# Block sums of the first 1024 tokens written straight into weight places, and single weight halves taken ahead of the last block

## The chip, the core and the metric

The kernel runs on one core of a Trainium2 chip. The metric is the device time of one execution in microseconds (us). TensorE (PE) does the matmuls, VectorE (DVE), ScalarE (ACT) and GpSimd (POOL) the elementwise work, and SyncE (SP) issues nearly all DMAs.

## What is computed

The reference has three stages in a row:

- a decaying linear attention over 4 sequences of 768 tokens, 8 heads of 64: state = gamma * state + k v^T, y = q state / 8. Its output is x, 3072 tokens by 512;
- layer 1: h = x @ w_in (512 to 2048), g = max(0.01 h, h), x2 = g @ w_out (2048 to 512);
- layer 2: h = x2 @ w_in2, g = h * cos(h), out = g @ w_out2, of the same sizes.

All of it is wanted at fp32 precision. A matmul operand is therefore split into a high part (rounded to the fp32r type) and a low part (the rest), and each product is three matmuls: high*high, low*high, high*low (`mm3`, lines 330 to 333).

## The kernel before

**Blocks and stages.** The 3072 tokens are six blocks of 512. Layer 1 runs over `SEGMENTS` (line 678): blocks 0 and 1 in two parts each, then n = 2, 3, 4, 5 whole. In a block, step f (0 to 15) does `gemm1` of 128 hidden features (12 matmuls), and then `gemm2_a` of step f-3 (12 matmuls), since up to two finished g wait in `pending`. After PE's gemm1 the value goes through ACT (`Leaky.begin`, then `high_g`) and DVE (`low_g`, line 541). The output of block n goes to DRAM tensors `x2d[n]`. Attention for the block after is woven into blocks up to n = 4; the last block, n = 5, has none.

**Layer 2** runs after that in 24 "quads" (lines 960 to 1005), eight for each superblock s of 1024 tokens (two blocks). It uses a 2 by 2 block scheme with seven products, P1 to P7, in the order P1, P6, P7, P5, P2, P4, P3. The left factors are sums of weight blocks, held per pair p in `w2i[p]` (DRAM) and loaded by `load_wi`; the right factors are sums of the x2 blocks, 14 tiles per superblock (seven names, two halves k), each a high part of 512 columns beside a low part of 512. They stand in `xt[j]`, in the places `w{j}_0` in which layer 1 has its input weights. Layer 2's output weights are rounded and split to `w2d[f]` (DRAM) and loaded by `load_wo`.

**Side work and its order.** Layer 2's operands are made while layer 1 runs. There are three kinds of such work, and every step of it has a *moment*, two per f: `agenda.run(2*(NF*(n-2)+f-START)+k)` in `tick` (line 800), with START = 4. Block n = 3 has moments 24 to 55, n = 4 has 56 to 87, and n = 5 has 88 to 119. Engines take their instructions in program order, so a moment fixes each engine's order.

- A **half** (`half(f)`, line 617) makes `w2d[f]`: one fetch of 512 KB, two ACT passes, three DVE passes (`clamp`, `fraction`, `top_bits`; lines 125, 128, 133), a POOL add (line 138), then `parts`: an ACT copy for the high part, a POOL subtraction for the low part, and a 256 KB write for each. It spans 7 moments, and the next begins 4 after it. Halves work in `cbuf`.
- A **pair** (`pair_at`, line 628) makes `w2i[p]`: two fetches of 512 KB, twice the rounding, four sums on DVE (`pair_sums`, line 266, 256 columns each), and four high and low parts, 1.8 MB of writes. Pairs 0 and 1 work in `cbuf`. Pairs 2 to 7 are those of `last_pairs`: they begin at moments 88, 92, ..., 108 in buffers of their own, the pool `ppool`, and take 10 moments each (the last ends at moment 118).
- **xprep** (line 276) makes the 14 x tiles of one superblock: for each k four fetches of 256 KB from `x2d` into `cbuf`, four sums on DVE, seven high parts on ACT (line 249), seven low parts on DVE (line 255), and a write of 256 KB to `xq[s]` for each part.

Before the change the order is: halves 0 to 7 (moments 0 to 34), pair 0 (32 to 44), xprep of s = 0 (46 to 70), pair 1 (69 to 81), halves 8 to 15 (80 to 114). So half 9's end and halves 10 to 15 run in the last block beside the six pairs. Also in the last block, `load_xq(0, f)` (line 813) brings one x tile of 512 KB from `xq[0]` back after each gemm1 of f = 0 to 13, `load_wo` brings 8 tiles of 512 KB, and `load_wi` 1.8 MB at f = 8 and again at f = 15.

**The crossing to layer 2.** `ppool` is closed and `bpool` opened in its room (line 842), so the first tile of `bpool` (`a`, copied by ACT at line 978 out of P1's bank) has to wait for the last DMA that reads a `ppool` tile. The products take their banks in turn: P1 and P6 two of `ps_h`, P7 `attA`, and P5 needs P1's bank again.

```python
650:            for f in range(8):
651:                half(f)
652:            pair(0)
653:            xprep(agenda, m + 3, 0)
654:            m += 26
655:            pair(1)
656:            for f in range(8, NF):
657:                half(f)
```

Of the kernel before, what the change touches and what calls it, by code (L numbers as in the profile page):

```python
# [12 lines left out]
F32 = mybir.dt.float32  # L13
F32R = mybir.dt.float32r
# [4 lines left out]
ALU = mybir.AluOpType  # L19
# [5 lines left out]
P = 128  # L25
# [7 lines left out]
NB = NT // BLK  # L33
# [24 lines left out]
WIN = 3584  # L58
WCOLS = {"P1": (0, 512), "P2": (256, 768), "P6": (1024, 1536), "P3": (1280, 1792), "P7": (2048, 2560), "P5": (2304, 2816), "P4": (3072, 3328)}
XORDER = ("P1", "P6", "P7", "P5", "P2", "P4", "P3")  # L60


def tables():
# [17 lines left out]
def body(ctx: ExitStack, tc: tile.TileContext, att, w1, w2, tab, out):  # L81
    nc = tc.nc
# [7 lines left out]
    dpool = ctx.enter_context(tc.tile_pool(name="dpool", bufs=1, space=DRAM))  # L90
# [19 lines left out]
    def w_tile(f, part, dt, n):  # L110
        return wpool.tile([P, n], dt, tag=f"w{f}_{part}", name=f"w{f}_{part}")
# [96 lines left out]

    w2d = [dpool.tile([P, 1024], F32, name=f"w2d{f}") for f in range(NF)]
    w2i = [dpool.tile([P, WIN], F32, name=f"w2i{p}") for p in range(NF // 2)]  # L210
    xq = [[dpool.tile([P, 1024], F32, name=f"xq{s}_{i}") for i in range(14)] for s in range(NB // 2)]
    made = set()


# [26 lines left out]

    def parts(t, dst, lo, eng, keep, out):

        o = []

        def high():
            n = t().shape[-1]
            o.append(out(n))
            nc.scalar.copy(out=o[0].bitcast(F32R), in_=t().bitcast(F32))
            nc.sync.dma_start(out=dst[:, lo : lo + n], in_=o[0])  # L250

        def low():
            n = t().shape[-1]
            w = out(n) if keep else t().bitcast(F32)
            eng.tensor_tensor(out=w.bitcast(F32R), in0=t().bitcast(F32), in1=o[0], op=ALU.subtract)
            nc.sync.dma_start(out=dst[:, lo + n : lo + 2 * n], in_=w)

        return high, low

# [13 lines left out]
    def done(*what):  # L273
        return lambda: made.add(what)

    def xprep(agenda, m, s):

        def place(i):
            return lambda: cbuf[:, i, :]

        def fetch(i, k):
            src = x2d[2 * s + i // 2][:, 2 * (i % 2) + k, :]
            nc.sync.dma_start(out=cbuf[:, i, :].bitcast(F32), in_=src)

        b11, b21, b12, b22 = (cbuf[:, i, :] for i in range(4))
        for k in range(2):
            way = {}
            for i, name, keep in ((0, "P1", True), (1, "P2", True), (3, "P3", True), (0, "P5", False), (2, "P7", False), (3, "P6", False), (1, "P4", False)):
                way[name] = parts(place(i), xq[s][2 * XORDER.index(name) + k], 0, nc.vector, keep, ostage)
            b = m + 13 * k  # L290
            for i in range(4):
                agenda.put(b + (0 if k == 0 else (-3, 0, -2, -1)[i]), partial(fetch, i, k))
            for j, name in ((2, "P1"), (3, "P2"), (4, "P3"), (6, "P5"), (7, "P7"), (8, "P6"), (9, "P4")):
                agenda.put(b + j, way[name][0])
                agenda.put(b + j + 1, way[name][1])
                if name == "P3":
                    agenda.put(b + 4, partial(sub2, b11, b12, b11))
                    agenda.put(b + 5, partial(sub2, b12, b22, b12))
                if name == "P5":
                    agenda.put(b + 6, partial(sub2, b22, b22, b11))  # L300
                    agenda.put(b + 7, partial(sub2, b21, b21, b22))
        agenda.put(m + 24, done("x", s))


    xt = {}

    def load_xq(s, j):
        assert ("x", s) in made
        xt[j] = w_tile(j, 0, F32R, 1024)
        nc.sync.dma_start(out=xt[j].bitcast(F32), in_=xq[s][j])  # L310

    wo = {}

# [230 lines left out]
    with tc.manual_schedule():  # L544

        with ExitStack() as pctx, ExitStack() as actx:
# [57 lines left out]
            agenda = Agenda()  # L604
            START, LAST = 4, 2 * (NF * (NB - 3) - 4)
# [11 lines left out]
            def half(f):  # L617
                nonlocal m, turn
                t = own(2 + turn % 2)
                turn += 1  # L620
                first, mid, last = rounding(raw2, t)
                high, low = parts(t, w2d[f], 0, nc.gpsimd, False, ostage)
                for i, step in enumerate((begin(f, 1), int, first, mid, last, high, low)):
                    agenda.put(m + i, step)
                agenda.put(m + 6, done("w", f))
                m += 4
# [15 lines left out]
            def pair(p):  # L642
                nonlocal m, turn
                t1, t2 = own(2 + turn % 2), own(3 - turn % 2)
                fetches = [begin(2 * p + i, 0) for i in range(2)]
                times = (0, 2, 3, 4, 4, 6, 7, 8, 5, 6, 9, 10, 10, 11, 11, 12, 12)
                pair_at(agenda, m, p, t1, t2, (raw2, raw2), fetches, times, (nc.gpsimd, nc.gpsimd, nc.vector), ostage, ostage)
                m += 11
# [1 line left out]
            for f in range(8):  # L650
                half(f)
            pair(0)
            xprep(agenda, m + 3, 0)
            m += 26
            pair(1)
            for f in range(8, NF):
                half(f)

            def last_pairs(ppool):
                def late(fn):  # L660
# [124 lines left out]
            for seg, (n, f0, f1) in enumerate(SEGMENTS):  # L785
                limit = LAG - 2 if seg < 4 else 1
                steps = list(PLAN[seg])
                size, at = len(steps), 0

                def slots(k):  # L790
                    for _ in range(size - len(steps), min(size, (k * size + size // 2) // (2 * (f1 - f0)))):
                        steps.pop(0)()

                def tick(k):
                    if seg < 4 and wa.busy() and k < int(TICKS[seg][f - f0]):
                        if loads and (seg > 0 or loads[0][0] < NF - 7):
                            load_w(1)
                        wa.tick()
                    if n > 1:
                        agenda.run(2 * (NF * (n - 2) + f - START) + k)  # L800

                for f in range(f0, f1):
                    if n == NB - 1 and f % 4 > 1:
                        hp = ps_att.tile([P, 512], F32, tag="attA" if f % 4 == 2 else "attB", name="hp")
                    else:
                        hp = ps_h.tile([P, 512], F32, tag="h", name="hp")
                    hp = hp[:, :BLK]
                    if len(pending) > limit:
                        need(wa, pending[0][2], 1)
                    need(wa, f, 0)  # L810
                    gemm1("a", f, xs[n], hp)
                    if n == NB - 1 and f < 14:
                        load_xq(0, f)
                    if n == NB - 1 and f == 8:
                        load_wi(0, 0)
                    if n == NB - 1 and f == NF - 1:
                        load_wi(1, 1)
                    if prev:
                        g = leaky.finish(*begun)
                        gh = high_g(g)  # L820
                    slots(2 * (f - f0) + 1)
                    tick(0)
                    second(limit)
                    if prev:
                        eng = nc.gpsimd if seg < 3 and GLP[seg][f - f0] == '1' else nc.vector
                        pending.append((gemm2_a, *prev[:2], low_g(g, gh, eng), *prev[2:]))
                    begun = leaky.begin(hp)
                    slots(2 * (f - f0) + 2)
                    tick(1)
                    prev = n, f, f0, f1  # L830
                if f1 == NF:
                    xs.pop(n)
                if n == NB - 2:
                    actx.close()
                    ppool = pctx.enter_context(tc.tile_pool(name="ppool", bufs=1))
                    last_pairs(ppool)
# [12 lines left out]
        def product(q, name):  # L849
            w = wi[pair_of(q)][0]  # L850
            hi, lo = WCOLS[name]
            at = XORDER.index(name)
            o = bank("attA") if (7 * q + at) % 3 == 2 else ps_h.tile([P, 512], F32, tag="h", name="hp")
            for k in range(2):
                j = 2 * at + k
                x = xt[j]
                mm3(o, w[:, hi + k * P : hi + k * P + P], w[:, lo + k * P : lo + k * P + P], x[:, :512], x[:, 512:], k == 0, k == 1)
                if q % NQ == NQ - 1 and q < QUADS - 1:
                    load_xq(q // NQ + 1, j)
            return o  # L860
# [86 lines left out]
        places = {f: f for f in range(8)}  # L947
        xagenda = Agenda()
        for s in range(1, NS):
            xprep(xagenda, 4 * NQ * (s - 1) + 1, s)  # L950
        moment = iter(range(4 * QUADS))

        def spare():
# [90 lines left out]
```

## Time and profile before

| | |
|---|---|
| median of 3 runs (range) | 1180.66 us (1179.08 to 1181.03) |
| the profiled execution | 1182.37 us, its span 1180.3 us |
| PE busy | 1129.1 us (96%), 5584 matmuls |
| DVE busy | 841.7 us (71%) |
| ACT busy | 525.9 us (45%) |
| POOL busy | 295.5 us (25%) |
| DMA moved | 204.82 MB, 174 GB/s over the span |
| mean granted TensorE clock | 0.991 |

The span is the time from the first to the last instruction in the trace; the execution's own time is 2.07 us more. The profile cuts the span into 40 slices of 29.5 us, with the busy share of each engine in tenths, the granted clock, and the DMA rate. A queue of DMA instructions on an engine is named SPq or ACTq.

### The profile page before, as it was taken

What the parts mean: (1) busy time and instruction counts of PE and PEld (TensorE: products, weight loads), DVE (VectorE), ACT (ScalarE), POOL (GpSimd) and SP (SyncE); (2) the same over time, 40 slices, a digit from 0 to 9 for tenths busy, and PEclk for the clock granted to TensorE, in tenths of its full rate; (3) what the DMA queues carried; (4) which work ended last, traced back from release to release, by engine and by line L of the source; (5) the groups of instructions that cost most, each with busy time, mean ns of one, the idle gap of its engine ahead of it and who ended that gap; (6) DMA issues with size and microseconds to landing.
All of it is one profiled execution on the core that took longest, in us unless ns stands there. A gap on an engine that the chain in (4) does not pass through costs nothing.

```text
span 1180.3 us, 15708 instructions
## 1 busy us (share of the span) xinstructions
PE 1129.1 (96%) x5584; PEld 929.6 (79%) x5584; DVE 841.7 (71%) x1313; ACT 525.9 (45%) x954; POOL 295.5 (25%) x274
## 2 busy tenths in 40 slices
PE   7889989999999999999987799999999999999998
PEld 5678778888888888888865577888888888888886
DVE  7899885444555655653797588798888897877875
ACT  4556543333334443334544354453445444444432
POOL 5687763222334421233455200000000000000000
PEclk9999999999999999999998899999999999999999
DMA  9905422223335344414999744648455567343321
GB/s 343 312 10 205 161 71 73 73 92 105 108 110 176 117 169 169 180 63 141 330 388 390 248 143 156 233 146 321 170 195 198 190 231 265 116 143 134 108 88 72
DMA packets 79854, 204.82 MB, mean 174 GB/s; under 512 B 8864, under 2 KB 13088, under 8 KB 79776
## 3 DMA queue, kind: packets, MB, share of 16 engines
q1 hardware_dynamic: 79632, 203.56, 48.9%
q8 instruction: 44, 0.72, 0.3%
q14 instruction: 34, 0.28, 0.1%
q10 hardware_dynamic: 144, 0.26, 0.1%
HBM read 144.02 MB, written 59.77 MB: 173 GB/s over the span
## 4 chain that ended last, share of the span: by engine, by line
PE 73%; DVE 14%; DMA 7%; ACT 2%; issue 2%; POOL 1%; SPq 1%; ACTq 0%; DVEq 0%; POOLq 0%
PE hp L331 9%; PE hp L333 9%; PE hp L332 9%; PE acc L331 9%; PE acc L333 9%; PE acc L332 9%; PE attB L331 3%; PE attB L332 3%; PE attB L333 3%; PE attA L331 2%; PE attA L333 2%; PE attA L332 2%; DVE cbuf L128 2%; DVE g L541 2%; DVE cbuf L133 2%
## 5 line engine op out<-in xcount | busy, mean ns | idle before, releaser
L333 PE MATMUL acc<-g,w 128*128 128x512 f32 x384 | 152.9, 398 | 12.4 <-DVE g L541 12.3
L331 PE MATMUL acc<-g,w 128*128 128x512 f32 x384 | 154.4, 402 | 4.6 <-ACT g L537 2.6
L331 PE MATMUL hp<-b,w 128*128 128x512 f32 x384 | 150.8, 393 | 5.4 <-ACT t L529 3.2
L332 PE MATMUL acc<-g,w 128*128 128x512 f32 x384 | 152.1, 396 | 0.0
L333 PE MATMUL hp<-b,w 128*128 128x512 f32 x384 | 150.1, 391 | 1.1 <-POOL b L509 1.0
L332 PE MATMUL hp<-b,w 128*128 128x512 f32 x384 | 149.8, 390 | 0.0
L882 ACT ACTIVATE r<-r,bias 128x512 f32<-128x512 f32 x96 | 69.6, 725 | 88.1 <-DVE r L881 88.1
L541 DVE TENSOR_TENSOR g<-t,g 128x512 fp32r<-128x512 f32 x91 | 88.6, 974 | 18.1 <-ACT g L537 17.4
L333 PEld LDWEIGHTS acc<-g,w 128*128 128x128 f32 x384 | 73.6, 192 | 30.3 <-DVE g L541 14.0
L331 PE MATMUL hp<-w,b 128*128 128x512 f32 x224 | 88.0, 393 | 8.2 <-ACT a L978 6.5
L331 PEld LDWEIGHTS acc<-g,w 128*128 128x128 f32 x384 | 73.5, 191 | 21.5 <-ACT g L537 3.0
L331 PEld LDWEIGHTS hp<-b,w 128*128 128x128 f32 x384 | 72.4, 189 | 21.9 <-ACT t L529 4.1
L333 PE MATMUL hp<-w,b 128*128 128x512 f32 x224 | 87.6, 391 | 0.0
L332 PE MATMUL hp<-w,b 128*128 128x512 f32 x224 | 87.6, 391 | 0.0
L333 PEld LDWEIGHTS hp<-b,w 128*128 128x128 f32 x384 | 72.2, 188 | 17.6 <-POOL b L509 2.4
L332 PEld LDWEIGHTS acc<-g,w 128*128 128x128 f32 x384 | 73.5, 191 | 14.1
L332 PEld LDWEIGHTS hp<-b,w 128*128 128x128 f32 x384 | 72.3, 188 | 14.3
L537 ACT CAST g<-t 128x512 fp32r<-128x512 f32 x96 | 59.4, 619 | 48.5 <-PE acc L333 47.5
L509 POOL TENSOR_TENSOR b<-xs,b 128x256 fp32r<-128x256 f32 x32 | 28.8, 899 | 189.7 <-ACT b L508 189.7
L332 PE MATMUL acc<-w,g 128*128 128x512 f32 x192 | 75.1, 391 | 1.1 <-DVE g L541 1.0
L333 PE MATMUL acc<-w,g 128*128 128x512 f32 x192 | 74.7, 389 | 0.0
L331 PE MATMUL acc<-w,g 128*128 128x512 f32 x192 | 74.7, 389 | 0.0
(194 smaller groups left out, 2526.2 us busy)
## 6 DMA issues: line engine op xcount, KB each, us to landing
b<-w2i SPq DMA_DIRECT2D x60, 512.0 KB, 5.5
w<-xq SPq DMA_DIRECT2D x42, 512.0 KB, 5.7
w<-w SPq DMA_DIRECT2D x32, 512.0 KB, 7.8
raw<-att SPq DMA_DIRECT2D x32, 512.0 KB, 4.5
w<-w2d SPq DMA_DIRECT2D x32, 512.0 KB, 8.0
xq<-o SPq DMA_DIRECT2D x60, 256.0 KB, 2.3
cbuf<-w SPq DMA_DIRECT2D x20, 512.0 KB, 4.0
w<-att SPq DMA_DIRECT2D x14, 512.0 KB, 7.6
```

The source lines that it names most:

```text
L128: nc.vector.tensor_scalar(out=t, in0=t, scalar1=3, scalar2=LOW_BITS, op0=ALU.logical_shift_left, op1=ALU.bitwise_and)
L133: nc.vector.scalar_tensor_tensor(out=t, in0=raw[:, :, 1], scalar=SIGN_TOP, in1=t, op0=ALU.bitwise_and, op1=ALU.bitwise_or)
L331: nc.tensor.matmul(o, sh, mh, start=start, stop=False)
L332: nc.tensor.matmul(o, sl, mh, start=False, stop=False)
L333: nc.tensor.matmul(o, sh, ml, start=False, stop=stop)
L509: nc.gpsimd.tensor_tensor(out=xl[dst], in0=xs, in1=xh[dst].bitcast(F32), op=ALU.subtract)
L537: nc.scalar.copy(out=pair[:, 0], in_=g)
L541: eng.tensor_tensor(out=pair[:, 1], in0=g, in1=pair[:, 0].bitcast(F32), op=ALU.subtract)
L882: nc.scalar.activation(out=r, in_=r, func=AF.Sin, bias=bias[:, 1:2], scale=1.0)
```

## The change

The x tiles of the first superblock are no longer written to DRAM and loaded again: ACT writes the high part and DVE the low part straight into the place `w{j}_0`, and `load_xq(0, f)` is gone. For that the work has to come when those places are free, so xprep of s = 0 moves to moment max(m + 3, LAST + 5) = 93, into the last block. Halves 8 to 15 come directly after pair 0, at moments 43 to 77, then pair 1 at 75 to 87. Tiles are numbered j = 7k + position in `XMADE`, the order in which they are made, so place j is written from moment 95 (j = 0) to moment 116 (j = 13). For s = 1 and 2 everything still goes through `xq`, and xprep of those begins one moment later than before.

```diff
+XMADE = ("P1", "P2", "P3", "P5", "P7", "P6", "P4")
...
-    xq = [[... for i in range(14)] for s in range(NB // 2)]
+    xq = [[... for i in range(14)] for s in range(1, NB // 2)]
...
         def high():
             n = t().shape[-1]
-            o.append(out(n))
+            o.append(out(n) if out else dst()[:, :n])
             nc.scalar.copy(out=o[0].bitcast(F32R), in_=t().bitcast(F32))
-            nc.sync.dma_start(out=dst[:, lo : lo + n], in_=o[0])
+            if out:
+                nc.sync.dma_start(out=dst[:, lo : lo + n], in_=o[0])
 
         def low():
             n = t().shape[-1]
-            w = out(n) if keep else t().bitcast(F32)
-            eng.tensor_tensor(out=w.bitcast(F32R), in0=t().bitcast(F32), in1=o[0], op=ALU.subtract)
-            nc.sync.dma_start(out=dst[:, lo + n : lo + 2 * n], in_=w)
+            w = (out(n) if keep else t().bitcast(F32)) if out else dst()[:, n:]
+            eng.tensor_tensor(out=w.bitcast(F32R), in0=t().bitcast(F32), in1=o[0].bitcast(F32), op=ALU.subtract)
+            if out:
+                nc.sync.dma_start(out=dst[:, lo + n : lo + 2 * n], in_=w)
...
-    def xprep(agenda, m, s):
+    def xprep(agenda, m, s, xlow=None):
...
-                way[name] = parts(place(i), xq[s][2 * XORDER.index(name) + k], 0, nc.vector, keep, ostage)
+                j = 7 * k + XMADE.index(name)
+                if s == 0:
+                    way[name] = parts(place(i), partial(own_x, j), 0, xlow or nc.vector, keep, None)
+                else:
+                    way[name] = parts(place(i), xq[s - 1][j], 0, nc.vector, keep, ostage)
...
+    def own_x(j):
+        if j not in xt:
+            xt[j] = w_tile(j, 0, F32R, 1024)
+        return xt[j]
...
             pair(0)
-            xprep(agenda, m + 3, 0)
-            m += 26
-            pair(1)
             for f in range(8, NF):
                 half(f)
+            pair(1)
+            xprep(agenda, max(m + 3, LAST + 5), 0)
...
                     gemm1("a", f, xs[n], hp)
-                    if n == NB - 1 and f < 14:
-                        load_xq(0, f)
...
-                j = 2 * at + k
+                j = 7 * k + XMADE.index(name)
...
-            xprep(xagenda, 4 * NQ * (s - 1) + 1, s)
+            xprep(xagenda, 4 * NQ * (s - 1) + 2, s)
```

## Rows read from the trace of the kernel before

**Rows 1.** The page: busy tenths and DMA rate in 40 slices of 29.5 us.
```profile
PE   7889989999999999999987799999999999999998
DMA  9905422223335344414999744648455567343321
GB/s 343 312 10 205 161 71 73 73 92 105 108 110 176 117 169 169 180 63 141 330 388 390 248 143 156 233 146 321 170 195 198 190 231 265 116 143 134 108 88 72
```

**Rows 2.** Stretches of 10 us: busy time (instructions) per engine, clock, DMA share, GB/s.
```profile
core 0: us, PE busy (x) PEld busy (x) DVE busy (x) ACT busy (x) POOL busy (x), PEclk, DMA share, GB/s
330.00:340.00 10.00, 10.00 (x49) 8.37 (x48) 5.95 (x9) 5.82 (x14) 6.45 (x7) 1.00 0.41 139
...
560.00:570.00 10.00, 10.00 (x46) 8.29 (x45) 6.15 (x11) 5.93 (x11) 2.62 (x2) 1.00 0.81 294
...
590.00:600.00 10.00, 8.38 (x37) 6.59 (x36) 9.65 (x13) 3.09 (x7) 5.68 (x4) 1.00 1.04 394
600.00:610.00 10.00, 9.18 (x34) 7.51 (x35) 9.83 (x12) 7.16 (x14) 6.99 (x5) 0.83 1.00 374
...
620.00:630.00 10.00, 7.17 (x31) 5.30 (x29) 5.14 (x9) 3.74 (x7) 5.00 (x5) 1.00 1.04 398
```

**Rows 3.** Waits, 540 to 700 us: total, times, longest; the last is SP's queue.
```profile
ACT t L120 <- DMA w2i<-t: 26.7, 4, 7.1
...
PE acc L333 <- DVE g L541: 12.3, 4, 4.0
...
PE hp L331 <- ACT a L978: 6.5, 2, 6.1
...
SPq L310 <- PE hp L333: 13.7, 4, 5.7
```

**Rows 4.** Timeline of PE: steps 0 and 6 of block 5, then the crossing.
```profile
551.52 0.39 PE L331 MATMUL hp<-b,w 128*128 128x512 f32 x1
...
584.16 0.39 PE L331 MATMUL hp<-b,w 128*128 128x512 f32 x1
...
600.82 0.80 PE L333 MATMUL acc<-g,w 128*128 128x512 f32 x1 [2.44 <-DVE g L541]
...
666.68 0.39 PE L333 MATMUL attA<-w,b 128*128 128x512 f32 x1
...
673.17 0.80 PE L331 MATMUL hp<-w,b 128*128 128x512 f32 x1 [6.11 <-ACT a L978]
...
680.07 0.40 PE L331 MATMUL hp<-w,b 128*128 128x512 f32 x1
```

**Rows 5.** Timeline of DVE, with one POOL instruction, in block 5.
```profile
558.15 0.69 DVE L541 TENSOR_TENSOR g<-t,g 128x512 fp32r<-128x512 f32 x1 [4.95 <-ACT g L537]
...
589.38 0.69 DVE L255 TENSOR_TENSOR t<-t,o 128x512 fp32r<-128x512 f32 x1
589.99 1.81 DVE L541 TENSOR_TENSOR g<-t,g 128x512 fp32r<-128x512 f32 x1
...
593.27 0.43 DVE L128 TENSOR_SCALAR cbuf<-cbuf 128x512 int32<-128x512 int32 x1
593.73 0.69 DVE L133 SCALAR_TENSOR_TENSOR cbuf<-cbuf 128x512 int32<-128x512 int32 x1
...
594.56 1.36 POOL L138 TENSOR_TENSOR cbuf<-cbuf 128x512 int32<-128x512 int32 x1 [1.60 <-DVE cbuf L133]
...
594.79 1.41 DVE L128 TENSOR_SCALAR t<-t 128x512 int32<-128x512 int32 x1
...
600.08 0.69 DVE L541 TENSOR_TENSOR g<-t,g 128x512 fp32r<-128x512 f32 x1
```

**Rows 6.** Timeline at the crossing: last low part of the pairs, its write, first bpool tile.
```profile
662.45 1.42 DVE L255 TENSOR_TENSOR t<-t,o 128x512 fp32r<-128x512 f32 x1 [0.61 <-ACT o L249]
...
664.87 0.46 SPq L256 DMA_DIRECT2D w2i<-t  x1
...
672.54 0.58 ACT L978 COPY a<-hp 128x512 f32<-128x512 f32 x1 [8.45 <-DMA cbuf<-x2d]
```

**Rows 7.** The page: DMA issues, count, size, median us to landing.
```profile
w<-xq SPq DMA_DIRECT2D x42, 512.0 KB, 5.7
...
xq<-o SPq DMA_DIRECT2D x60, 256.0 KB, 2.3
```

More of the change, by code (lines that the diff above doesn't have):

```diff
@@ L210, in body @@
     w2i = [dpool.tile([P, WIN], F32, name=f"w2i{p}") for p in range(NF // 2)]
-    xq = [[dpool.tile([P, 1024], F32, name=f"xq{s}_{i}") for i in range(14)] for s in range(NB // 2)]
+    xq = [[dpool.tile([P, 1024], F32, name=f"xq{s}_{i}") for i in range(14)] for s in range(1, NB // 2)]
     made = set()
@@ L309, in load_xq @@
         xt[j] = w_tile(j, 0, F32R, 1024)
-        nc.sync.dma_start(out=xt[j].bitcast(F32), in_=xq[s][j])
+        nc.sync.dma_start(out=xt[j].bitcast(F32), in_=xq[s - 1][j])
+    def own_x(j):
+        if j not in xt:
+            xt[j] = w_tile(j, 0, F32R, 1024)
+        return xt[j]
     wo = {}
```

## The prediction

> **What bounds the kernel now.** I read the page's slices first, then stretches of 10 us around the weak place, then the waits there, then PE's and DVE's own timelines. The slices show a PE that is busy nine tenths or more in the middle of the run, with one dip at slices 22 and 23 (649 to 708 us), and a DMA share of nine tenths and more in slices 19 to 21 (560 to 649 us), at 330 to 390 GB/s [rows 1]. That is the last layer-1 block and the crossing to layer 2. In stretches of 10 us the DMA engines, at a share of 0.81 from 560, are full from 590 on (1.00 to 1.04, 374 to 398 GB/s), DVE is busy 9.65 and 9.83 us of 10 in two of them, and PE has gaps and in one a clock of 0.83 [rows 2]. In the blocks before, PE is busy for 10.00 of 10 us, also at 330 us, where halves 0 to 7 run beside attention [rows 2]; no wait of PE is listed between 200 and 550 us. So what the change does to the earlier blocks lies under PE, and its worth is what it does to block 5.
>
> How much there is to win: PE starts step 0 at 551.52 and step 6 at 584.16, so a full-speed step is 32.64 / 6 = 5.44 us, or 0.227 us for each of its 24 matmuls [rows 4]. From 584.16, ten more steps and 30 matmuls (P1, P6, a gemm2, P7) would bring P5 to 584.16 + 54.4 + 6.8 = 645.4; it starts at 673.17. The 18 matmuls from there to 680.07 take 6.90 us and not 4.1 [rows 4]. **The loss is 27.8 + 2.8 = 30.6 us**, the most that this change can bring.
>
> Two things make it. One is DMA: PE's waits in the block are for DVE's low part of g (12.3 us), behind ACT, which stands 26.7 us in four waits for writes from the pairs' `t2` buffers to land, and at the end PE waits 6.1 us for the ACT copy into `a` [rows 3, 4]. SP itself stands 13.7 us in front of the 14 x loads until PE has freed their places [rows 3], and the fetches behind them in SP's order stand too. The other is DVE: the low part of g of step 0 runs 1.2 us after step 1 begins (558.15 against 556.96), that of step 5 at 600.08, which is 14.7 us later than step 6's start plus the same 1.2, and only then does PE stop, for 2.44 us [rows 4, 5]. **DVE may thus lag PE by about 12.5 us before it costs anything.**
>
> **Part 1: the x tiles no longer pass through DRAM.** It removes 14 loads of 512 KB (5.7 us to landing, [rows 7]) from block 5 and 28 writes of 256 KB (2.3 us) from the middle blocks. The writes were under PE: nothing. The loads are 7.3 MB, 18.6 us of full DMA at 395 GB/s [rows 2], and SP's stand of 13.7 us goes with them.
>
> **Part 2: halves leave block 5, xprep enters.** Six and a half halves take away 6.8 MB (fetch and two writes), 13 POOL instructions and 20 DVE passes; xprep adds eight fetches, 2.1 MB, 14 ACT copies in place of about 20 ACT passes, and 22 DVE instructions. Pairs 17.3 MB, `load_wo` 4.2, `load_wi` 3.7 and block 4's output 1.05 stay. Bytes: 38.5 MB before fall to 28.3 MB. Before, 38.5 / 0.395 = 97 us from 562 gives 659, just where layer 2 began. After, 28.3 MB need 72 us: **DMA no longer bounds the block**, though the part of it up to moment 108 asks some 20 MB in 43.5 us, 50 us of transfer, so fetches can still be late by up to 7 us there.
>
> **What is late next: DVE.** One two-input pass costs 0.61 us from start to start (589.38 to 589.99), a fast one-input pass 0.46 (593.27 to 593.73), a set of three roundings 1.53; a POOL instruction beside them costs DVE about 1.0 us (1.41 for 0.43) [rows 5]. For the 256-wide sums I take 0.46. From moment 95, about 570.5 us, the changed block has on DVE: 10 rounding sets, 15.3; six times sums and the narrow low part, 13.8; six more low parts, 3.7; 12 low parts of g, 7.3; xprep 22 x 0.61 = 13.4; 21 POOL instructions, 21. That is 74.5 us, against 65 us of PE for moments 95 to 118. The lag grows to 9 us at the end; laid out by moment it peaks near 13 at moment 114, just at the tolerance. So PE loses perhaps 0 to 5 us within the block, and DVE ends the pairs at about 570.5 + 74.5 = 645.
>
> The crossing then is a chain: DVE's last low part, its write, the landing, ACT's copy, P5. Before: 663.87, issue 664.87 with a second write behind, copy at 672.54 [rows 6], since 1.8 MB of `load_wi` and a full queue stand in front. After, `load_wi` is issued near 636 to 641 and done by 645, so I take about 3.5 us from low part to landing (2.3 us is the nearest undisturbed landing of that size, [rows 7]; 8.7 us is what it takes now). P5 starts at about 649. I add 3 us for stalls that in-order engines pass to each other (bounds 0 and 7, the late fetches): **P5 near 652, 21 us earlier than 673.17.** The slow-clock stretch after the wait (2.8 us) I leave as it is, since a wait of 3 us or more remains.
>
> **Part 3: halves 8 to 15 move to moments 43 to 77,** past SP's and POOL's attention work, in place of xprep (22 DVE instructions). Per half POOL gets 2 x 1.4 us. The same mix runs at 330 us with POOL at 6.45 of 10 us and PE at 10.00 [rows 2]: nothing, as long as POOL is not full. **Part 4: the later xprep begin one moment later,** the same work under the same quads: nothing, between -1 and +1 us.
>
> **Sum.** 1182.37 - 21 = 1161.4 for the execution profiled, whose time stands 1.71 us above the median: **1159.7 us.**
>
> Here the notes and the rows can differ in one term. The rows have a POOL pass of 1.36 us delay a DVE pass by 0.98 us [rows 5]. The Trainium skill, "SBUF — State Buffer", section Terms, says that the two engines share a port pair by an exclusive lock for a whole instruction, so that the loser blocks completely. By that DVE would pay 1.36 for each of the 21, 8 us more, and the time would be 1168. The rows decide, since most collisions begin inside POOL's pass.
>
> **Rivals.**
>
> *A, everything is covered.* POOL and DVE collide less in the thinner stream, DVE never lags by 12.5 us, and the write lands before P5 wants its bank: 30.6 us, 1150. For: before, POOL often ran while DVE stood. Against: 74.5 us of DVE in 65. Chance 0.10 for 1150 to 1153.
>
> *B, DVE stays the bound.* Collisions cost 1.36 us, or fetches come 7 us late: P5 at 660 to 667, so 1168 to 1175. For: DVE at 9.65 and 9.83 of 10 us [rows 2]. Chance 0.13.
>
> *C, the removed transfers were hidden anyway.* Each x load was issued tens of us before a product read it, and if other waits kept their length, the time would stay: 1180.7. Against: SP's 13.7 us and DMA shares over 1.0 [rows 2, 3]. The Trainium skill, "DMA: Bandwidth & Descriptors", Rules for kernel authors, says that a load issued early and waited for late overlaps. By that rule taking it out wins nothing; the trace agrees for the load itself, not for what queues behind it. Chance 0.04.
>
> *D, slower: the halves reach PE in the attention blocks.* Place: moments 43 to 77, some 410 to 520 us. Price: eight halves, each 2 x 1.4 us of POOL and two DVE collisions of 1.0, 38 us in all, if every one delays the key and x low parts that attention's matmuls need. Then 1159.7 + 38 = 1198. It decides, against the gain of 21, once over 21/38 = 55% of it is exposed. Against: PE at 10.00 with that mix [rows 2]. Chance 0.05.
>
> **How the numbers follow.** The forecast, 1153 to 1168, has 0.68; A 0.10, B 0.13, C 0.04, D 0.05. A range of 1150 to 1171 takes the forecast, A, and about half of B, 0.84. A measurement of this kernel tells 0.2% (2.4 us) from no change. Faster is forecast, A and B, 0.91; within 0.2% is C, 0.04; slower is D, 0.05.
>
> **What would show it.** In the profile after: DMA share in block 5 clearly under 1 for most of it and SP's wait for PE gone; layer 2's first product near 640 to 645 and P5 near 650; the low part of g still late by 8 to 13 us around steps 12 to 14; PE's remaining waits for that low part, and for the copy into `a`; no PE wait between 200 and 550 us. It would be wrong if DVE is idle in the block, waiting for fetches (DMA still the bound), if DVE is full and PE waits for it as long as now, or if PE shows gaps at 410 to 520 us.

## The result and the profile after

The kernel after takes 1167.3 us (median of 4 runs, 1165.62 to 1168.09) against 1180.85 us (4 runs, 1179.08 to 1181.18): a ratio of 0.9886, with a 95% interval of 0.9869 to 0.9904, or 13.5 us less. The profiled execution took 1168.09 us, its span 1166.3 us; 190.14 MB were moved instead of 204.82. The time lies 7.6 us above the predicted 1159.7 and inside the range.

In the page of after, PE's busy tenths, the DMA share and the rate over 40 slices of 29.2 us:

```profile
PE   6989989999999999999997799999999999999998
DMA  9906413122334433432588455549556557343321
GB/s 346 316 3 214 164 39 106 55 91 90 126 128 145 141 131 118 164 108 91 198 298 307 163 180 190 198 162 346 187 170 219 187 209 261 118 144 136 116 84 73
```

The dip of PE is still there, in slices 21 and 22, and the plateau of DMA in front of it has gone from 330 to 390 GB/s [rows 1] to 198, 298 and 307. Stretches of after in the columns of [rows 2], 130 us of the attention blocks first, then block 5:

```profile
410.00:540.00 130.00, 130.00 (x731) 109.61 (x730) 70.62 (x124) 56.24 (x113) 53.84 (x49) 1.00 0.37 124
...
570.00:650.00 80.00, 71.78 (x304) 57.68 (x303) 72.83 (x98) 42.51 (x80) 35.21 (x22) 0.98 0.84 292
...
570.00:580.00 10.00, 10.00 (x46) 8.27 (x45) 9.69 (x14) 4.73 (x9) 4.69 (x3) 1.00 0.96 315
...
610.00:620.00 10.00, 10.00 (x46) 8.29 (x45) 5.49 (x8) 3.08 (x7) 4.68 (x3) 1.00 1.02 366
620.00:630.00 10.00, 7.02 (x23) 4.99 (x22) 8.72 (x15) 6.05 (x13) 2.77 (x2) 0.83 1.02 400
```

The halves that moved into the attention blocks cost PE nothing there (130.00 of 130 us, as before the change). In block 5 DVE is full (9.69 of 10 us) wherever it is fed, but from 610 to 620 it has only 5.49 us of work while the DMA share is 1.02: it is short of data once, late in the block. Waits of after from 540 to 700 us (total, times, longest), against [rows 3]:

```profile
ACT t L121 <- DMA raw<-w: 10.8, 4, 6.9
ACT t L121 <- DMA w2i<-t: 9.8, 3, 4.0
...
PE acc L346 <- DVE g L554: 8.1, 4, 2.9
...
PE hp L344 <- ACT a L988: 4.1, 1, 4.1
```

ACT's waits for the pairs' writes fell from 26.7 to 9.8 us, PE's for DVE's g from 12.3 to 8.1, and SP's stand for the x places is gone. One of ACT's waits grew: the one for the pairs' fetches, the first line, which in before was

```profile
ACT t L120 <- DMA raw<-w: 3.4, 4, 1.6
```

PE's timeline of after, with block 5's step 0, its longest wait for g, P5 and P2:

```profile
553.01 0.39 PE L344 MATMUL hp<-b,w 128*128 128x512 f32 x1
...
624.88 0.50 PE L346 MATMUL acc<-g,w 128*128 128x512 f32 x1 [2.89 <-DVE g L554]
...
664.07 0.79 PE L344 MATMUL hp<-w,b 128*128 128x512 f32 x1 [4.12 <-ACT a L988]
...
669.58 0.39 PE L344 MATMUL hp<-w,b 128*128 128x512 f32 x1
```

Against [rows 4], the 14.0 us of the span come from these pieces. Step 0 starts 1.5 us later (553.01 against 551.52), which is scatter from run to run: in the profiles of the ten kernels that have the new order it starts between 551.21 and 553.35. From there to P5 it is 111.06 us where it was 121.65: 10.6 less. P5 to P2 takes 5.51 us where it was 6.90: 1.4 less. From P2 to the end it is 496.7 us where it was 500.2: 3.5 less, and that piece had not been forecast.

Two places of after explain what is left. The first is a late fetch; SP's queue, ACT and DVE from 605 us:

```profile
605.62 3.60 SPq L341 DMA_DIRECT2D b<-w2i  x4
...
610.49 0.57 SPq L230 DMA_DIRECT2D raw<-w  x1
...
618.70 0.66 ACT L121 ACTIVATE t<-raw 128x512 f32<-128x512 f32 x1 [6.92 <-DMA raw<-w]
...
619.39 0.43 DVE L126 TENSOR_SCALAR t<-t 128x512 f32<-128x512 f32 x1 [4.41 <-ACT t L121]
```

`load_wi` of f = 8, 1.8 MB that layer 2 needs 40 us later, is issued just ahead of a pair's fetch; that fetch keeps ACT waiting 6.92 us, DVE idles 4.41 us, and PE's wait of 2.89 us follows. The second is the crossing; DVE, SP's queue and ACT:

```profile
653.03 0.83 SPq L253 DMA_DIRECT2D w2i<-o  x2
653.55 1.44 DVE L258 TENSOR_TENSOR t<-t,o 128x512 fp32r<-128x512 f32 x1 [0.61 <-ACT o L251]
653.95 1.90 SPq L341 DMA_DIRECT2D b<-w2i  x4
...
655.95 1.17 SPq L260 DMA_DIRECT2D w2i<-t  x2
...
663.43 0.58 ACT L988 COPY a<-hp 128x512 f32<-128x512 f32 x1 [8.25 <-DMA w2i<-t]
```

The last low part ends at 654.99, but SP is issuing the second `load_wi`, so the write that holds the room of `a` goes out at 655.95 behind it, and `a` is copied 8.4 us after the low part.

### The profile page after: what moved, and what is told of

It is laid out like the page before. It is cut to its first block, busy times and chain, and to the rows that moved or that the text cites. A ratio compares the mean times of both kernels' runs of the same rounds, so it can differ in the third digit from the quotient of the medians.

```text
span 1166.3 us, 15608 instructions
## 1 busy us (share of the span) xinstructions
PE 1127.2 (97%) x5584; PEld 929.2 (80%) x5584; DVE 838.4 (72%) x1313; ACT 525.7 (45%) x954; POOL 296.7 (25%) x274
## 2 busy tenths in 40 slices
DMA packets 73807, 190.14 MB, mean 163 GB/s; under 512 B 8193, under 2 KB 12417, under 8 KB 73729
## 5 line engine op out<-in xcount | busy, mean ns | idle before, releaser
L346 PEld LDWEIGHTS acc<-g,w 128*128 128x128 f32 x384 | 72.7, 189 | 25.8 <-DVE g L554 9.8
L344 PEld LDWEIGHTS hp<-b,w 128*128 128x128 f32 x384 | 72.6, 189 | 20.7 <-ACT t L542 4.0
L344 PEld LDWEIGHTS acc<-g,w 128*128 128x128 f32 x384 | 72.5, 189 | 18.7 <-DVE o L752 1.9
L345 PEld LDWEIGHTS acc<-g,w 128*128 128x128 f32 x384 | 72.7, 189 | 13.8
L542 ACT ACTIVATE t<-hp 128x512 f32<-128x512 f32 x96 | 57.0, 594 | 34.4 <-PE hp L346 30.6
```

The costliest lines, as they stand in the source:

```text
L344: nc.tensor.matmul(o, sh, mh, start=start, stop=False)
L345: nc.tensor.matmul(o, sl, mh, start=False, stop=False)
L346: nc.tensor.matmul(o, sh, ml, start=False, stop=stop)
L542: nc.scalar.activation(out=t, in_=hp, func=AF.Prelu, alpha=0.01)
```

## The experiments

The theory: the removed bytes let fetches and writes land sooner; the rest of the loss is DVE's sum of work plus the two loads of written weights in the wrong place. The rivals: SP's stand was what mattered; the loads were hidden; the move of the halves did it. All times, with the gain over before as (1 - ratio) x 1181 us, and from each profile the time from block 5's step 0 to P5, which leaves out when the block starts:

| kernel | median us | ratio, 95% interval | gain us | step 0 to P5, us |
|---|---|---|---|---|
| before | 1180.85 | | | 121.65 |
| after | 1167.3 | 0.9886 (0.9869 to 0.9904) | 13.5 | 111.06 |
| e1_noload | 1170.96 | 0.9909 (0.9893 to 0.9925) | 10.7 | 111.20 |
| e8_copies | 1180.28 | 0.9992 (0.998 to 1.0003) | 0.9 | 121.96 |
| e9_xag1 | 1170.74 | 0.9909 (0.9894 to 0.9924) | 10.7 | 110.60 |
| e2_dummy | 1172.83 | 0.9926 (0.9908 to 0.9943) | 8.7 | 115.26 |
| e3_nosums | 1159.97 | 0.9828 (0.9803 to 0.9854) | 20.3 | 103.09 |
| e7_pool_low | 1173.18 | 0.9917 (0.9898 to 0.9936) | 9.8 | 115.49 |
| e4_wi1_late | 1159.75 | 0.9814 (0.9798 to 0.9831) | 22.0 | 106.72 |
| e5_wi0_early | 1164.06 | 0.9849 (0.9832 to 0.9865) | 17.8 | 106.27 |
| e6_both | 1156.26 | 0.9785 (0.9771 to 0.98) | 25.4 | 100.74 |
| e10_halves_late | 1162.17 | 0.9825 (0.9806 to 0.9844) | 20.7 | 108.43 |
| e11_x_earlier | 1157.45 | 0.978 (0.9756 to 0.9804) | 26.0 | 102.87 |
| e12_xag3 | 1157.63 | 0.9792 (0.9775 to 0.9809) | 24.6 | 100.68 |

**e1_noload: part 1 alone, on the kernel before.**

```diff
-                        load_xq(0, f)
+                        xt[f] = wslot["a", f, 0]
```

> The kernel before, with only the 14 x loads of the last block left out: the products of the first superblock read layer 1's old input weights as if they were x, so the output differs. Everything else, the halves in the last block too, stays. If the bytes of the loads and SP's stand in front of them were what the change won by, this alone gives most of the change's 13.5 us: 1167 to 1171. If DVE, with the halves and POOL beside it, is what holds PE in the last block, the loads alone give little: 1177 to 1181. If both act in turn, as the prediction had it, about half: 1172 to 1176.

It gained 10.7 us: leaving the loads out is most of the change.

**e8_copies: the loads' bytes kept, SP's wait for their places taken away.** On the kernel before; each x load becomes a copy to a scrap tensor in DRAM, and layer 1's weights stand in for x.

```diff
-                        load_xq(0, f)
+                        xt[f] = wslot["a", f, 0]
+                        nc.sync.dma_start(out=scrap[f], in_=xq[0][f])
```

> The kernel before, with each of the 14 x loads replaced by a copy of the same 512 KB tile from DRAM to a spare DRAM tensor at the same place; layer 1's old weights stand in for x, so the output differs. The bytes stay, SP's stand until PE frees a place goes. Leaving the loads out gave 1171.0. If the bytes are the cost, this stays near the kernel before: 1176 to 1181. If SP's stand of 13.7 us and the fetches behind it are the cost, it comes near 1171: 1170 to 1174.

No difference from before that can be told, although SP no longer waits for PE there. DVE's busy time from 570 to 650 us is 63.55 us, where it was 64.35 before and 72.83 in after:

```profile
570.00:650.00 80.00, 67.30 (x272) 53.36 (x270) 63.55 (x84) 37.62 (x70) 42.29 (x29) 0.93 0.98 365
```

So it was the transfers and not SP's stand. One reserve: a copy also writes DRAM, which a load does not. The load on the DMA engines was no higher for it, a share of 0.98 and 365 GB/s in that stretch against 1.01 and 377 in before.

**e2_dummy: bytes put back into the kernel after,** 14 copies of 512 KB that nothing waits for.

```diff
+                    if n == NB - 1 and f < 14:
+                        nc.sync.dma_start(out=scrap[f], in_=w2d[f % 8])
```

> The changed kernel with 14 copies of 512 KB from DRAM to DRAM put where the x loads stood, one at each f from 0 to 13 of the last block, for nothing: DMA traffic comes back, but no wait for PE and no work on DVE. If DMA load was the main loss before, the time goes up by 8 to 13 us, to 1175 to 1180. If DVE is the bound now and DMA has room, by 0 to 3 us, to 1167 to 1170.

It gave back 5.5 us by the medians, between the two cases expected and about half of what e1 gained. In 620 to 630 us DVE has 5.77 us of work and PE 5.12, with DMA at 412 GB/s:

```profile
620.00:630.00 10.00, 5.12 (x19) 3.52 (x18) 5.77 (x10) 3.03 (x6) 1.36 (x1) 0.81 1.04 412
```

**e9_xag1: the kernel after with the later xprep at their old moment.**

```diff
-            xprep(xagenda, 4 * NQ * (s - 1) + 2, s)
+            xprep(xagenda, 4 * NQ * (s - 1) + 1, s)
```

> The changed kernel with the later x preparation back at its old moment (one earlier). In the first four quads PE was busy 57.1 of 60 us after the change and 55.1 before. If the one-moment shift is the reason, 2 to 4 us are lost again: 1169 to 1171.5. If it is nothing, as the prediction had it: 1166 to 1168.5.

It lost 3.4 us by the medians; the two intervals overlap slightly, so the place in the trace has to tell. P2 starts at 668.21 in e9, and from there to the end (span 1168.2) it is 500.0 us, 3.3 more than in after. PE's waits behind P5 in the quads of e9 and then of after:

```profile
PE attA L344 <- ACT a L988: 1.7, 1, 1.7
PE hp L344 <- DVE c L873: 1.6, 1, 1.6
PE acc L345 <- DVE g L554: 1.0, 1, 1.0
```

```profile
PE attA L344 <- ACT a L988: 1.2, 1, 1.2
PE acc L345 <- DVE g L554: 1.0, 1, 1.0
PE hp L344 <- DVE c L873: 0.8, 1, 0.8
```

DVE shows why, in e9 and then in after:

```profile
688.06 0.68 DVE L258 TENSOR_TENSOR o<-cbuf,o 128x512 fp32r<-128x512 f32 x1
688.66 0.68 DVE L873 TENSOR_TENSOR a<-attA,a 128x512 f32<-128x512 f32 x1
```

```profile
688.30 0.68 DVE L554 TENSOR_TENSOR w<-r,w 128x512 fp32r<-128x512 f32 x1
689.24 0.69 DVE L873 TENSOR_TENSOR a<-attA,a 128x512 f32<-128x512 f32 x1 [0.26 <-PE attA L346]
```

In e9 a low part of xprep stands ahead of the quad's own sum in DVE's order; in after that sum comes straight behind its product. Just behind the crossing DVE has little slack (46.51 us busy of the 52 from 668 to 720 in after), and one moment decides which goes first. All waits of PE listed behind P5 come to 6.0 us in e9 and 3.6 in after, so these rows place 2.4 of the 3.3 us.

Set beside e1, e9 is the whole change but the shift, and e1 only part 1, and both gained 10.7 us. So the move of the halves, with xprep in their place, seemed to be worth nothing. Two lines from 540 to 700 us, of e1 and then of e9, suggest that a gain was given back:

```profile
PE acc L333 <- DVE g L541: 9.1, 4, 4.2
...
PE hp L331 <- ACT a L978: 2.8, 2, 2.4
```

```profile
PE hp L344 <- ACT a L988: 6.8, 2, 6.3
...
PE acc L346 <- DVE g L554: 5.9, 4, 2.7
```

PE waited 3.2 us less for g, and then 4.0 us more for `a`: P5 started at 662.40 in e1 and at 661.87 in e9. What was won in the block was waited away at the crossing.

**e4_wi1_late: the kernel after with the second `load_wi` behind the last pair's writes.**

```diff
-                    if n == NB - 1 and f == NF - 1:
-                        load_wi(1, 1)
...
                     tick(1)
+                    if n == NB - 1 and f == NF - 1:
+                        load_wi(1, 1)
```

> The changed kernel with the second load of weight sums (1.8 MB, four DMAs) issued after the last pair's two writes and not right before them. In the changed kernel these writes took 6.6 us to land, and the first tile of the next pool waited for them. If it is the transfer in front that makes them late, they land in about 2.5 us, P5 starts some 4 us earlier, and the time is 1162 to 1164. Rival: the load itself is then late for quad 1, or the wait only moves to another tile of the new pool: 1166 to 1169.

DVE, SP's queue and ACT at the crossing of e4:

```profile
651.68 1.43 DVE L258 TENSOR_TENSOR t<-t,o 128x512 fp32r<-128x512 f32 x1 [0.60 <-ACT o L251]
652.59 0.87 SPq L260 DMA_DIRECT2D w2i<-t  x2
653.54 1.91 SPq L341 DMA_DIRECT2D b<-w2i  x4
655.85 0.59 ACT L988 COPY a<-hp 128x512 f32<-128x512 f32 x1 [2.53 <-DMA w2i<-t]
```

The same two instructions of SP in the other order: the last low part ends at 653.11 (651.68 + 1.43), the copy follows at 655.85, 2.7 us later and not 8.4, and PE doesn't wait for it. By the medians 7.6 us are gained from moving one call, more than was expected. The profiles place some 5.8 of them: 4.34 from step 0 to P5, and 1.43 behind it (P5 to P2 takes 4.08 us and not 5.51).

**e5_wi0_early: the kernel after with the first `load_wi` at f = 0,** where DMA is free (a share of 0.44 from 550 to 570 us of after).

```diff
-                    if n == NB - 1 and f == 8:
+                    if n == NB - 1 and f == 0:
                         load_wi(0, 0)
```

> The changed kernel with the first load of weight sums (1.8 MB) at f = 0 of the last block in place of f = 8. Around f = 10 ACT stood 6.9 us for a pair's fetch and DVE then idled 4.4 us, with the DMA share at 1.02 and that load just in front. If the load is what makes the fetch late, DVE's gap shrinks and the block ends 2 to 5 us earlier: 1162 to 1165.5. If DVE's own sum is what counts and the gap is slack, nothing: 1166 to 1168.

DVE's hole is filled (9.66 in 610 to 620 us, against 5.49) and PE's waits for g fall to 4.2 us, but part of it goes to the crossing again: its wait for `a` is 5.6 us against 4.1.

```profile
610.00:620.00 10.00, 10.00 (x45) 8.27 (x45) 9.66 (x12) 4.81 (x10) 5.93 (x4) 1.00 1.04 411
```

**e6_both: e4 and e5 together.**

> The changed kernel with both moves of the loads of weight sums: the first at f = 0, the second after the last pair's writes. If the late fetch and the late write are separate costs, their gains add: 1154.5 to 1158, below the 1159.75 of the second alone. If DVE bounds the end whatever the fetches do, the same as the second alone: 1159 to 1160.5.

At 1156.26 us it has the lowest median of the study, with nothing left out of the work: 25.4 us under before, 11.9 under after by the ratios. The two gains add, as the first case had it. No wait for `a` is left at the crossing, and these are PE's longest waits from 640 us on (the one for `a` is a later quad's):

```profile
PE acc L346 <- DVE g L554: 2.1, 1, 2.1
PE attA L344 <- ACT a L988: 1.2, 1, 1.2
PE acc L345 <- DVE g L554: 1.0, 1, 1.0
PE hp L344 <- DVE c L873: 0.8, 1, 0.8
```

**e10_halves_late: e6 without the move of the halves.** It is e1 with the edits of e4 and e5 and the later xprep at + 2.

> The kernel before with the x loads left out, with both loads of written weights moved as in e4 and e5, and with the later regroupings of x two moments behind their fetch: everything that e6 has but the move of the one-at-a-time weight halves, which stay in the last block, so that block 5 has 6.5 halves to prepare and no regrouping of stage 0's x. If moving the halves out is worth nothing because the regrouping of x that takes their place costs DVE as much (the reading of e1 against e9): 1155.5 to 1158, as e6's 1156.3. If that move is worth something that the late fetch and the late copy hid in e9: 1160 to 1166. If the halves in the last block are the better place: under 1155.

With both loads moved, the move of the halves shows: e6 is 4.7 us faster by the ratios. PE's waits for g are 9.2 us against 4.2 in e6:

```profile
PE acc L333 <- DVE g L541: 9.2, 3, 3.7
```

**e3_nosums: less DVE work.** The kernel after without the four sums of each of the last six pairs.

```diff
-lambda: pair_sums(t1(), t2()),
+(lambda: pair_sums(t1(), t2())) if p < 2 else int,
```

> The changed kernel without the four sums of each of the last six pairs (24 narrow DVE passes, 6 x 1.85 = 11 us of DVE; layer 2's weight sums and with them the output differ). No DMA changes. If DVE is the bound of the last block, it ends 6 to 10 us earlier: 1157 to 1161. If late fetches (DMA) are the bound, at most 2 us: 1165 to 1167.

7.3 us gained from leaving out some 11 us of DVE, with no DMA changed, and with DVE still short of work from 610 to 620 us (4.96 of 10): what DVE has to do costs time beside the late fetch. The sums also stand ahead of the pairs' last writes, so the run doesn't separate DVE's total from the length of each pair's chain.

**e7_pool_low: low parts of stage 0's x on POOL instead of DVE,** in the kernel after.

```diff
-            xprep(agenda, max(m + 3, LAST + 5), 0)
+            xprep(agenda, max(m + 3, LAST + 5), 0, nc.gpsimd)
```

> The kernel after with the subtractions that make the low parts of stage 0's x on POOL instead of DVE: some 14 operations and 8.5 us off DVE, 14 passes onto POOL. If DVE's own sum of work is what holds block 5 and a POOL pass costs DVE nothing: 1161 to 1164, PE's waits for DVE's g from 8.1 us to under 4. If each POOL pass takes about 1 us from DVE as the rows of before suggest, and lies on the chain behind it: 1167 to 1173, with DVE's mean per operation up in 570 to 650.

Slower than after by 5.9 us by the medians (the intervals touch), and by 4.4 from step 0 to P5 in the profiles. Groups by line of 570 to 650 us (busy, mean ns, idle before), of after and then of e7:

```profile
L258 DVE TENSOR_TENSOR w<-cbuf,w 128x512 fp32r<-128x512 f32 x14 | 10.6, 763 | 0.0
...
L126 DVE TENSOR_SCALAR t<-t 128x512 f32<-128x512 f32 x11 | 6.8, 622 | 5.4 <-ACT t L121 5.4
L129 DVE TENSOR_SCALAR t<-t 128x512 int32<-128x512 int32 x11 | 6.7, 605 | 0.4
```

```profile
L129 DVE TENSOR_SCALAR t<-t 128x512 int32<-128x512 int32 x11 | 10.6, 959 | 0.4
L126 DVE TENSOR_SCALAR t<-t 128x512 f32<-128x512 f32 x11 | 10.1, 921 | 4.8 <-ACT t L121 4.8
...
L258 POOL TENSOR_TENSOR w<-cbuf,w 128x512 fp32r<-128x512 f32 x12 | 18.1, 1513 | 6.9 <-ACT w L251 6.9
```

DVE lost 10.6 us of low parts, and its busy time didn't move: 73.08 us for 82 instructions instead of 72.83 for 98. At after's mean of each form those that remained would be about 11.5 us shorter: 11.5 / 12, some 0.96 us of DVE for each of these POOL passes of 1.51 us, or 1.05 by the 11 that POOL had more in all (33 against 22). The prediction's 1.0, from one pair of rows, holds. The Trainium skill, "SBUF — State Buffer", Terms, says that the shared port pair is held for the full instruction and that the loser "fully blocks". The trace agrees, but the price is not a whole pass: in before, from 551 to 665 us, all 29 DVE passes that the timeline lists singly and that ran more than 0.15 us over their short time (0.43 or 0.69 us) began inside a POOL pass, and on the average of e7's rows DVE lost about two thirds of one.

**e11_x_earlier and e12_xag3: moving work of e6 by a moment or two.**

```diff
-            xprep(agenda, max(m + 3, LAST + 5), 0)
+            xprep(agenda, LAST + 3, 0)
...
-            b = m + 13 * k
+            b = m + (13 if s else 15) * k
...
-        agenda.put(m + 24, done("x", s))
+        agenda.put(m + (24 if s else 26), done("x", s))
```

> e6 with the first half of the regrouping of stage 0's x begun at moment 91 instead of 93; the second half unchanged. If DVE's lag behind the products is what is left of the loss in block 5 (PE's waits for DVE's g of 4.2 us in e6), two moments more for the same work take most of it away: 1152 to 1155, PE's waits for g under 1.5 us. If the lag is set by what comes after moment 106, the second half and the last pairs: 1155.5 to 1157, the waits unchanged.

```diff
-            xprep(xagenda, 4 * NQ * (s - 1) + 2, s)
+            xprep(xagenda, 4 * NQ * (s - 1) + 3, s)
```

> e6 with the regroupings of x for superblocks 1 and 2 begun three moments behind the start of the superblock before instead of two. If the 3.4 us that the shift from one to two was worth come from DVE work of the regrouping that stands before the sums of the first quads, one more moment takes some of what is left there (PE's waits behind the crossing of 1.2, 1.0, 0.8 and 0.5 us in e6): 1153.5 to 1155.5. If those waits are the quads' own, and the shift from one to two had already cleared them: 1155.5 to 1157, the waits unchanged. If the regrouping now ends too near to the quads that load it: 1158 to 1163, with new waits near the next superblock's start.

Neither can be told from e6, and both medians lie just above the ranges that stood for no change. In e11 PE waited 6.2 us for g, not less than 4.2. In e12 the wait for `c` fell from 0.8 to 0.2, but two for DVE's `w` grew from 0.5 to 1.8. What e6 still loses in block 5 isn't settled by these; e3 makes DVE's sum the likely holder.

## Why the prediction came out 7.6 us low

**Part 1, right in what it removes, wrong in one reason.** The loads were the main thing: leaving them out gains 10.7 us alone, where the change gains 13.5 (e1), against 18.6 us of transfer. Of the two reasons given, the bytes hold, and SP's stand of 13.7 us was worth nothing that can be told (e8).

**Part 2, "DMA no longer bounds the block".** Right for most of it, and "fetches can still be late by up to 7 us" was met by one of 6.92 us. Its bytes hold: 259 GB/s over the 110 us from 550 to 660 are 28.5 MB, where 28.3 were forecast. For before, the terms that it names add to 40.4 MB and not 38.5 (102 us at that rate and not 97); only its check of the rate on before rests on that, not the forecast. The 3 us added for passed-on stalls was too little. With them DVE should have ended the pairs 96.5 us after step 0 (645 + 3 - 551.52); it took 101.98 (654.99 - 553.01), 5.5 more. DVE's work was sized well: in the last 82.99 us of that, counted as in the prediction from 19 us after step 0, it was busy for 75.08, and 74.5 had been forecast. It stood for 7.9 us and not 3. Most of that, 5.4 us by the row of L126 above, is behind ACT's first pass on a pair's tile, and 4.41 us of it is the hole of the late fetch, which e5 fills. The prediction had `load_wi` of f = 15 in view, but did not look at what that of f = 8 is queued ahead of.

**The crossing, the term that was mis-sized.** The prediction took 3.5 us from low part to landing, because "`load_wi` is issued near 636 to 641 and done by 645". It was issued at 653.95, since SP takes its instructions in order and stood in front of it for the late writes of line 253: a load placed by its step is as late as the waits ahead of it. Low part to copy was 8.4 us, and to P5 9.1 us where 4 were taken: 5.1 more. With the load behind the write low part to copy is 2.7 us (e4), so the 3.5 was sound for an undisturbed chain. 5.5 + 5.1 is the 10.6 us by which step 0 to P5 (111.06 us) was longer than forecast (652 - 551.5 = 100.5).

**The slow-clock stretch** was left at 2.8 us. Behind the wait for `a`, P5's matmuls start 0.43 us apart, at the lower of the clock's two levels (1.2 GHz), and later ones 0.23 us apart, at the upper (2.4 GHz). In before that stretch followed a wait of 6.1 us, in after one of 4.1 us, and it cost 1.4 us and not 2.8 (P5 to P2, 5.51 us against 4.1 at the upper level). The granted clock is the column of 0.66 and 0.83 here, for before from 670 to 680 us and for after from 660 to 670:

```profile
670.00:680.00 10.00, 6.83 (x18) 5.38 (x19) 4.06 (x6) 2.03 (x3) 0.00 (x0) 0.66 0.42 161
```

```profile
660.00:670.00 10.00, 5.93 (x20) 4.83 (x21) 4.06 (x6) 1.34 (x3) 0.00 (x0) 0.83 0.24 85
```

**Part 3, right.** PE was busy for 130.00 of 130 us from 410 to 540, so rival D falls.

**Part 4, "nothing, between -1 and +1 us", wrong.** It was worth about 3.3 us (e9): the same work under the same quads, but ahead of the quad's own sums in DVE's order where DVE is late. The profiled span fell by 14.0 us where 21 had been forecast: 10.6 too much up to P5 and 1.5 of a later step 0, less 1.4 and 3.5 gained behind P5, is the 7 us by which it missed. So part of the nearness was luck: 3.5 us came from a term that had been put at nothing, and without it the kernel takes 1170.74 us (e9), outside the forecast of 1153 to 1168 and just inside the range of 1150 to 1171.

**The rivals.** A falls. B, which had DVE still the bound, fetches 7 us late and P5 at 660 to 667, describes what happened better than the forecast did: P5 started at 664.07. Only the gains behind P5 keep the time just under its 1168. e3 points to DVE's work as a bound, and e5 shows that one late fetch adds to it. C falls with e1. The Trainium skill, "DMA: Bandwidth & Descriptors", Rules for kernel authors, says of a DMA issued early and waited for late that "the fixed setup cost overlaps". The trace agrees for the 14 loads themselves, since no wait of PE for one is listed in before, but taking them out was still worth 10.7 us, and e8 puts that on the transfers.

## What to carry to other kernels

When loads are taken off a full queue, look at what is left in issue order at each place where an engine must have a landing: a load that is needed late but issued just ahead of a fetch or write that is needed now can put its transfer on the critical path, and moving two such calls was worth nearly as much here (11.9 us) as the change itself. An edit that measures as nothing may have had its gain taken by the next wait, so try it again with that wait removed. Where an in-order engine has no slack, shifting side work by one position is an edit to be costed, not a detail.

## What was not expected

Moving 10.6 us of subtractions from DVE to a POOL that was busy for 35.21 of 80 us bought DVE nothing: the passes it kept grew by as much in sum (two of the forms from 622 to 921 ns and from 605 to 959 ns). And the move of the halves measured 0.0 us with the two loads where they were (e1 against e9), and 4.7 us with both moved (e10 against e6).
